# A fused forward and backward kernel with its order planned in advance: first loads, first norm, PSUM places of the last stage and output stores changed

## The chip, the cores and the metric

The kernel runs on one core of a Trainium2 chip. A core has TensorE (PE, matrix products into PSUM), VectorE (DVE), ScalarE (ACT), GpSimd (POOL) and SyncE (SP, which here only issues transfers). PSUM, where PE writes, is 128 partitions wide and is used here as eight places (banks) of 2 KB in each partition. Working memory beside it is one large "slab" that the kernel divides itself. Transfers are carried out by 16 DMA engines; they are issued on the queues of SP, ACT or POOL.

The metric is the device time of one execution in microseconds (us), the median of several runs. A profile is one such execution, recorded instruction by instruction; its span goes from the first to the last instruction.

## The reference

All arrays are bf16; the sequence has S = 2048 tokens of D = 512 channels, the hidden width is F = 1376. The forward pass normalizes the tokens and uses the result twice, in a long convolution and in a gated layer:

```python
xn = _layernorm(q)
k_shift = sum of 4 shifted copies of k, each times one tap of shift_k (per channel)
kv = k_shift * v
y  = irfft(rfft(kv padded to 4096) * rfft(ssm_k padded to 4096))[:2048] + kv * ssm_D
s  = xn * y
h  = sigmoid(xn @ w_gate) * (xn @ w_up)
out = q + s * silu(h @ w_down)
```

The result is `out` and the gradients of q, k, v, shift_k, ssm_k, ssm_D, w_gate, w_up and w_down for a given `grad_out`, so ten outputs (`out_0` to `out_9`).

## The kernel before, in words

**Tiles and stages.** Tokens are handled in 8 groups of 256 (`q` in the code), channels in 4 groups of 128 (`cg`). The Fourier transform of 4096 points is done by small matmuls (`step1n`, `step3` forward, `inv3`, `inv3w`, `inv1`, `inv1n` back). There are three stages:

1. Three streams side by side: `strG` (norm of the tokens in `f_ln`, its transposes in `f_Tpe` and `f_T`, gate and up products in `f_gen`), `strK` (the filter's transform) and `strV` (the four taps on k as matmuls with diagonal matrices `dg4`, the product with v, its transform, the product with the filter's and the way back).
2. `stepB`: the gated layer's output and its backward pass, token group by token group.
3. Behind the last groups of it: `dW` (the three weight gradients, in blocks of 16 matmuls of 128x512, 128x352 or 128x320 that accumulate in one PSUM place each), `frontC` (transform of the convolution's incoming gradient) and `backC` with `taps` (products with the stored transforms, the way back, and the gradients of k, v, the taps and the filter). `dW` reads chunks of stored activations by transposing loads on SP's queue; `backC` reads stored transforms (`KK_d`).

**The order.** The functions don't issue instructions. They record them in `Rec`, with what each depends on. `run_streams` interleaves the streams' records by a share of progress, and `Rec.order` then lays out all engines' instructions with estimated durations: at each step the engine that is free first takes the lowest-numbered recorded operation that is ready. PSUM tiles get their place there. A tile has a kind, and `KINDS` (L175) lists the sets of places that a kind may take; of the free sets the one that has been free longest is taken, and an operation whose tile finds none is put back. For a four-place tile that finds none, the planner holds places as they come free. The kinds that matter here:

- `m2`: two places, (4,5), (6,7), (2,3) or (0,1); used by `step1n` (L794), `step3` (L815) and `inv1` (L856), and by much of stages 1 and 2.
- `f4`: four places, 0 to 3 or 4 to 7; used by `inv3w` (L827), `inv3` (L841) and `inv1n` (L871).
- `f4a`: 0 to 3 alone. No tile of the kernel before has this kind.
- `hi`: one of 4 to 7; the accumulators of `dW`.
- `m1`: any single place.

The result is one fixed program; each engine works through its part in that order and waits at semaphores.

**The first microseconds.** `f_x(0)` (L939) loads the first 256 tokens as two halves of 64 partitions on SP's queue, and the first gate and up weights go out on ACT's queue behind nothing (L940). `gen_fft_consts` records the Fourier matrices' angles on DVE in two halves of a loop, and their sines on ACT; the generator hands over behind the loop. Then `f_ln(0)` is recorded: for each of two 128-token tiles statistics, their aggregate, an add of the epsilon, a power of -0.5 on POOL, and the normalizing product. `f_Tpe(0)` transposes by matmul. The rest of the constants waits for the second tile's statistics by an added dependency (`ln0`), the second group's norm for the first one's end. The diagonal matrices `dg4` of channel group 0 (L1062) need the taps, which POOL loads.

**The last outputs.** The gradient of v (`out_3`) is a product in `taps` for each channel group, in place in `y2A`; the gradient of k (`out_2`) is in `stC["v"]`. Both are stored behind the last channel group, in four row groups of two halves each: eight stores for each output, all 512 columns at a time.

In the profile nearly every instruction carries line L566 (PE) or L568 (all others), where recorded operations are issued, so groups are told apart by engine, operation and shape.

Of the kernel before, what the change touches and what calls it, by code (L numbers as in the profile page):

```python
# [17 lines left out]
P = 128  # L18
# [6 lines left out]
NJ = 16  # L25
# [138 lines left out]
class Rec:  # L164
# [8 lines left out]
    hold = None  # L173
    ENGS = ("tensor", "vector", "scalar", "gpsimd", "sync")
    KINDS = {"f4": [(0, 1, 2, 3), (4, 5, 6, 7)], "m2": [(4, 5), (6, 7), (2, 3), (0, 1)],  # L175
             "g2": [(4, 5), (6, 7), (2, 3)], "z2": [(4, 5), (6, 7)], "f4a": [(0, 1, 2, 3)], "lo": [(0,), (1,), (2,), (3,)],
             "hi": [(4,), (5,), (6,), (7,)], "m1": [(7,), (6,), (5,), (4,), (3,), (2,), (1,), (0,)]}

    def __init__(self, nc, tc, slab, psum):
# [418 lines left out]
def gen_fft_consts(nc, ar, negpi, Cn, TT, RT, I32):  # L598
    sc = 2 * math.pi / 8192
    rings = []  # L600

    def tmp(shape, dt):
        r = Ring(ar, shape, dt)
        rings.append(r)
        return r.ap
    a = tmp([16], i32)
    nc.gpsimd.iota(a, pattern=[[1, 16]], base=0, channel_multiplier=32)
    b = tmp([64], i32)
    nc.gpsimd.iota(b, pattern=[[2, 64]], base=1, channel_multiplier=0)
    pi_ = tmp([4], i32)  # L610
    nc.gpsimd.iota(pi_[:, 0:1], pattern=[[0, 1]], base=0, channel_multiplier=1)
    x32 = tmp([32], f32)
    nc.gpsimd.iota(x32, pattern=[[1, 32]], base=0, channel_multiplier=0, allow_small_or_imprecise_dtypes=True)
    yield
    nc.vector.tensor_single_scalar(a[64:128], a[64:128], -2032, ALU.add)
    m = tmp([8, 64], i32)
    mc = tmp([16, 2, 2, 32], i32)
    mv = m.rearrange("p j (h l) -> p j h l", h=2)
    for j in (slice(0, 8), slice(8, 16)):
        nc.vector.tensor_tensor(m, a[:, j, None].to_broadcast([P, 8, 64]), b[:, None, :].to_broadcast([P, 8, 64]), ALU.mult)  # L620
        nc.vector.tensor_single_scalar(mc[:, j, :, 1], mv, 8191, ALU.bitwise_and)
        nc.vector.tensor_single_scalar(m, m, 6144, ALU.add)
        nc.vector.tensor_single_scalar(mc[:, j, :, 0], mv, 8191, ALU.bitwise_and)
        nc.scalar.activation(Cn[:, j], mc[:, j].rearrange("p j h c l -> p j (h c l)"), ACT.Sin, bias=negpi, scale=sc)
    yield
    nc.vector.tensor_single_scalar(pi_[:, 1:2], pi_[:, 0:1], 31, ALU.bitwise_and)
    nc.vector.tensor_single_scalar(pi_[:, 2:3], pi_[:, 0:1], 5, ALU.arith_shift_right)
    nc.vector.tensor_single_scalar(pi_[:, 2:3], pi_[:, 2:3], 1, ALU.bitwise_and)
    pf = tmp([4], f32)
    nc.vector.tensor_copy(pf[:, 0:2], pi_[:, 1:3])  # L630
    nc.vector.tensor_scalar(pf[:, 2:3], pf[:, 1:2], -8.0, 24.0, ALU.mult, ALU.add)
    nc.vector.tensor_single_scalar(pf[:, 3:4], pf[:, 1:2], 24.0, ALU.mult)
    nc.vector.tensor_scalar(I32, x32, pf[:, 0:1], None, ALU.is_equal)
# [12 lines left out]
    for r in rings:  # L646
        r.free()
    yield
# [11 lines left out]
def kernel_impl(ctx, tc, A_q, A_k, A_v, A_shift_k, A_ssm_k, A_ssm_D, B_x, B_w_gate, B_w_up, B_w_down,  # L660
# [66 lines left out]

    T = [dict() for _ in range(8)]
    flags = set()


    def f_x(q):
# [2 lines left out]

    def f_ln(q):
        xq = T[q]["xq"]
        for t in range(2):
            i = 2 * q + t
            st = lnst.next()  # L740
            nc.vector.bn_stats(st[:, 0:6], xq[:, t])
            nc.vector.bn_aggr(st[:, 6:8], st[:, 0:6])
            nc.vector.tensor_scalar_add(st[:, 8:9], st[:, 7:8], LN_EPS)
            nc.gpsimd.tensor_tensor(out=rstd_all[:, i:i + 1], in0=st[:, 8:9], in1=neghalf, op=ALU.pow)
            nc.vector.tensor_scalar(xnA[:, i, :], xq[:, t], st[:, 6:7], rstd_all[:, i:i + 1], ALU.subtract, ALU.mult)

    def f_T(q):
        T[q]["xnT"] = xnT_r.next()
# [41 lines left out]
    def step1n(src):  # L790
        V = V_r.next()
        Vv = V.rearrange("p w (r j) e -> p r j w e", r=2)
        for jq in range(4):
            ps = nc.ps("m2", [2, 4, GW], f32)  # L794
# [17 lines left out]

    def step3(U, X):
        for c in range(2):
            ps = nc.ps("m2", [2, 16, 32], f32)  # L815
            calls = []
            for t in range(4):
                for k in range(2):
# [5 lines left out]
            nc.evac(X[:, c].rearrange("p (x k l) -> p x k l", k=2, l=32), ps[:].rearrange("p k x l -> p x k l"), 1024)  # L824

    def inv3w(parts, u, B):
        ps = nc.ps("f4", [2, 8, 2, 64], f32)  # L827
        calls = []
        for w in range(8):
            for n, (Y, R) in enumerate(parts):  # L830
# [22 lines left out]

    def inv1(B, dst):
        for jq in range(4):
            ps = nc.ps("m2", [2, 4, GW], f32)  # L856
            calls = []
            for j in range(4 * jq, 4 * jq + 4):
                for c in range(2):
# [8 lines left out]
            yield 4096  # L868

    def inv1n(B, dst):  # L870
        ps = nc.ps("f4", [32, 64], f32)  # L871
        for jh in range(2):
            for j8 in range(2):
                calls = []
# [61 lines left out]
    nc.gpsimd.memset(wu[:, :, F:FP], 0.0)  # L936
    nc.vector.memset(negpi, -math.pi)
    nc.vector.memset(neghalf, -0.5)
    f_x(0)  # L939
    ld_w(nc.scalar, 0, 512)  # L940
    nc.gpsimd.dma_start(skT, A_shift_k.rearrange("(cg p) t -> p cg t", p=P))
    nc.gpsimd.dma_start(Dcol_b, A_ssm_D.rearrange("(cg p) -> p cg", p=P))
# [8 lines left out]
    for op in rec.ops[n0:]:  # L951
        op.deps.add(n0 - 2)
    next(consts)
    ln0 = len(rec.ops) + 5
    f_ln(0)
    f_Tpe(0)
    f_x(2)
    n0 = len(rec.ops)
# [20 lines left out]
    def strG():  # L979
        for q in range(8):  # L980
            if q == 0:
                n0 = len(rec.ops)
                f_ln(1)
                rec.ops[n0].deps.add(ln0 + 4)
                f_Tpe(1)
            if q + 2 < 8:
                f_ln(q + 2)
# [68 lines left out]
    def strV():  # L1056
        for cg in range(NG):
# [3 lines left out]
            kvt = vg[:, :, c0 % 256:c0 % 256 + GW]  # L1061
            nc.vector.tensor_tensor(dg4, ident[:, None, :].to_broadcast([P, 4, GW]),  # L1062
                                    skT[:, cg, :, None].to_broadcast([P, 4, GW]), ALU.mult)
            kTp = kTp_r.next()
            for r in range(2):
                o = 13 + 16 * r
# [341 lines left out]
    def taps(cg):  # L1408
# [10 lines left out]
        nc.vector.tensor_tensor(dkv, dkv, stC["ksh"], ALU.mult)  # L1419
        if cg + 1 < NG:  # L1420
            ld_ksh(cg + 1)
        else:
            for j in range(0, NJ, 4):
                dma2o(nc.sync, o3C[:, :, j:j + 4], y2A[:, j:j + 4])
        yield 512
        pa = nc.ps("m1", [4, 32], f32)
        calls = []
# [10 lines left out]
        for lag in range(4):  # L1438
# [6 lines left out]
                nc.vector.tensor_tensor(term, src, skl, ALU.mult)  # L1445
                nc.vector.tensor_tensor(dk, dk, term, ALU.add)
            yield 512
        if cg + 1 == NG:
            for j in range(0, NJ, 4):
                dma2o(nc.sync, o2C[:, :, j:j + 4], stC["v"][:, j:j + 4])  # L1450

    def endC():
        yield from backC()
# [15 lines left out]
    def gated(g, flag):  # L1469
        yield from g  # L1470
        flags.add(flag)
    live = run_streams([(gated(stepB(), "B"), 8 * 45056, 0.0, 1.0)], until=lambda: "d2" in flags)
    Lfree.append(L0_r)
    ld_L()
# [114 lines left out]
```

## Time and profile before

| what | value |
|---|---|
| median of 3 runs | 505.53 us (501.62 to 507.21) |
| the profiled execution | 500.71 us |
| its span | 498.9 us |
| mean granted TensorE clock in it | 0.986 |
| PE busy | 461.0 us, 92% of the span |
| DVE busy | 391.1 us, 78% |
| ACT busy | 276.6 us, 55% |
| POOL busy | 21.0 us, 4% |
| moved by DMA | 112.74 MB, mean 226 GB/s |

Shares of busy time are means over stages; the prediction goes by stages. In rows of the timeline the columns are start and busy time in us, engine, line, operation, what is written and read with shape and type, the count, and in brackets how long the engine was idle just before and what ended it. SPq, ACTq and POOLq are the queues' issuing instructions. In rows of grouped instructions the columns are busy us, mean ns of one, and idle time before them with what ended it.

### The profile page before, as it was taken

How to read it: one execution, taken by the hardware profiler on the slowest of the kernel's cores; microseconds unless marked ns; L12 is line 12 of the kernel's file. 1: busy time of each engine (PE TensorE's matmuls, PEld its weight loads, DVE VectorE, ACT ScalarE, POOL GpSimd, SP SyncE). 2: the span in 40 equal slices, each digit the busy share in tenths (PEclk: the TensorE clock that was granted, in tenths of full speed). 3: DMA queues.
4: the chain of work that ended last, by engine and by line, in shares of the span. 5: the costliest groups of instructions: out<-in, count | busy, mean ns of one | idle time of the engine just before them, and what ended most of it. 6: DMA issues, size and time to landing. Idle time of an engine off the chain costs nothing.

```text
span 498.9 us, 13661 instructions
## 1 busy us (share of the span) xinstructions
PE 461.0 (92%) x5862; PEld 303.7 (61%) x5895; DVE 391.1 (78%) x658; ACT 276.6 (55%) x346; POOL 21.0 (4%) x48
## 2 busy tenths in 40 slices
PE   3999989999999999999999999999899879969997
PEld 2686866686768655565566556445446556657665
DVE  6788979758867499978998998649777779985870
ACT  5659798667665674255355267146556745254121
POOL 4010110000000000000000000100000000000000
PEclk9799999999999999999999999999989999998999
DMA  9999989927399897998969788996989998984666
GB/s 251 214 258 290 298 226 266 276 111 223 146 269 260 209 265 129 293 279 261 285 195 267 197 197 208 218 264 225 180 214 250 248 204 235 221 190 140 163 211 203
DMA packets 173813, 112.74 MB, mean 226 GB/s; under 512 B 101621, under 2 KB 157881, under 8 KB 173752
## 3 DMA queue, kind: packets, MB, share of 16 engines
q1 hardware_dynamic: 172344, 110.42, 87.0%
q10 hardware_dynamic: 1056, 1.05, 0.8%
q8 instruction: 46, 0.75, 0.6%
q0 software_dynamic: 352, 0.40, 0.3%
q14 instruction: 15, 0.12, 0.1%
HBM read 39.23 MB, written 47.62 MB: 174 GB/s over the span
## 4 chain that ended last, share of the span: by engine, by line
PE 71%; DVE 12%; issue 6%; ACT 6%; DMA 4%; POOL 1%; ACTq 0%; DVEq 0%; POOLq 0%
PE psum L566 71%; DVE slab L568 12%; ACT slab L568 6%; DMA slab<-slab 3%; DMA slab<-in_A_shift_k_dram 1%; POOL slab L568 1%; PE psum L568 0%; ACTq L568 0%; DVEq L568 0%; POOLq L568 0%; POOLq L1573 0%
## 5 line engine op out<-in xcount | busy, mean ns | idle before, releaser
L566 PE MATMUL psum<-slab 64*128 64x128 bf16 (+10 forms) x5853 | 459.6, 266 | 34.5 <-ACT slab L568 16.9
L566 PEld LDWEIGHTS <-slab 128*128 128x128 bf16 (+5 forms) x5886 | 303.0, 103 | 190.5 <-issue 55.7
L568 ACT CAST slab<-psum 128x1024 bf16<-128x1024 f32 (+4 forms) x265 | 218.2, 875 | 170.5 <-PE psum L566 153.6
L568 DVE TENSOR_TENSOR slab<-slab 128x1024 bf16<-128x1024 bf16 (+4 forms) x344 | 242.8, 758 | 30.6 <-ACT slab L568 12.7
L568 DVE CAST slab<-psum 128x1024 bf16<-128x1024 f32 (+1 forms) x29 | 34.1, 1183 | 28.4 <-PE psum L566 14.8
L568 ACT ACTIVATE slab<-psum 128x1024 bf16<-128x1024 f32 (+2 forms) x44 | 37.4, 855 | 30.3 <-PE psum L566 28.9
L568 DVE TENSOR_TENSOR slab<-psum,slab 128x1024 bf16<-128x1024 f32 (+2 forms) x28 | 28.1, 1004 | 16.6 <-PE psum L566 14.1
L568 DVE STREAM_TRANSPOSE slab<-slab 128x512 f32<-128x512 f32 x48 | 30.8, 684 | 3.4 <-ACT slab L568 3.2
L568 ACT ACTIVATE slab<-slab 128x512 bf16<-128x512 bf16 (+3 forms) x25 | 21.8, 889 | 16.9 <-DVE slab L568 16.8
L568 DVE SCALAR_TENSOR_TENSOR slab<-slab 128x512 bf16<-128x512 bf16 (+1 forms) x48 | 24.7, 529 | 3.8 <-ACT slab L568 3.4
L568 DVE TENSOR_SCALAR slab<-slab 128x1 f32<-128x1 f32 (+8 forms) x58 | 14.0, 270 | 2.6 <-POOL slab L568 1.8
L568 POOL TENSOR_TENSOR slab<-slab 128x1 f32<-128x1 f32 (+1 forms) x20 | 9.9, 508 | 74.9 <-DVE slab L568 66.9
L568 POOL MEMSET slab<- 128x128 bf16 (+3 forms) x7 | 3.1, 446 | 219.6 <-PE psum L566 176.2
L568 DVE BATCH_NORM_STATS2 slab<-slab 128x6 f32<-128x512 bf16 x16 | 10.3, 677 | 1.9 <-DMA slab<-in_A_q_dram 1.9
L568 POOL DMA_DIRECT2D slab<-slab x8 | 4.3, 536 | 148.6 <-DVE slab L568 148.6
L568 DVE SCALAR_TENSOR_TENSOR slab<-psum,slab 128x512 bf16<-128x512 f32 x10 | 6.7, 684 | 3.2 <-PE psum L566 3.2
L568 DVE COPY slab<-slab 128x1216 bf16<-128x1216 bf16 (+2 forms) x17 | 7.2, 441 | 0.0
L568 ACT ACT_TABLE_LOAD x2 | 2.6, 1283 | 1.8 <-issue 1.8
L568 DVE MEMSET slab<- 32x192 uint32 (+3 forms) x8 | 1.3, 165 | 1.9 <-PEq L1573 0.8
L568 DVE BATCH_NORM_AGGREGATE slab<-slab 128x2 f32<-128x6 f32 x16 | 2.5, 170 | 0.0
L568 PE MATMUL psum<-slab 128*4 128x128 bf16 (+1 forms) x9 | 1.7, 331 | 0.0
L568 POOL DMA_DIRECT2D slab<-in_A_shift_k_dram x2 | 1.5, 762 | 3.2 <-DMA sF_d<-slab 3.2
(15 smaller groups left out, 9.6 us busy)
## 6 DMA issues: line engine op xcount, KB each, us to landing
KK_d<-slab SPq DMA_DIRECT2D x16, 512.0 KB, 3.7
slab<-KK_d SPq DMA_DIRECT2D x16, 512.0 KB, 4.7
out_dram<-slab SPq DMA_DIRECT2D x58, 128.0 KB, 3.5
hS_d<-slab SPq DMA_DIRECT2D x8, 704.0 KB, 6.2
dgS_d<-slab SPq DMA_DIRECT2D x8, 704.0 KB, 5.9
duS_d<-slab SPq DMA_DIRECT2D x8, 704.0 KB, 5.4
sF_d<-slab SPq DMA_DIRECT2D x6, 704.0 KB, 5.3
slab<-sF_d SPq DMA_DIRECT2D x6, 704.0 KB, 6.1
```

What stands on the lines that cost most here:

```text
L566: getattr(self.nc.tensor, m)(*[place(v) for v in aa], **{x: place(v) for x, v in kk.items()})
L568: getattr(getattr(self.nc, eng), meth)(*[place(v) for v in a], **{x: place(v) for x, v in k.items()})
```

## The change

It has four parts, and helpers for them.

- *First loads.* The two halves of the first 256 tokens are issued as the first transfer on SP's queue and the first on ACT's.
- *First norm.* `f_ln` handles its two tiles together: both statistics, then both aggregates and adds (the sum with the epsilon now goes into `rstd_all` itself), one power for two columns on POOL, and two products. The constants' generator hands over in the middle of its loop too, and its second half is recorded behind `f_ln(0)`. `dg4` of channel group 0 gets a dependency on the first norm's last product. The numbers added to `ln0` follow the new order inside `f_ln`; they name the same operations as before (second tile's statistics, last product).
- *PSUM places of the last stage.* `step1n`, `step3` and `inv1` take their kind from `two["k"]`: `m2` as before in stage 1, and a new kind `c2`, (6,7), (2,3) or (0,1), for what is recorded from `stepB` on. `inv3w` and `inv1n` take `f4a`.
- *Stores in column halves.* `taps` stores 256 columns of both outputs behind each second channel group, in two row groups of two halves: four stores of 256 KB for each output behind channel group 1 and four behind group 3.

```diff
+            "c2": [(6, 7), (2, 3), (0, 1)], "g2": [(4, 5), (6, 7), (2, 3)], ...
...
         nc.scalar.activation(Cn[:, j], mc[:, j].rearrange("p j h c l -> p j (h c l)"), ACT.Sin, bias=negpi, scale=sc)
-    yield
+        yield
...
+    two = {"k": "m2"}
...
     def f_ln(q):
         xq = T[q]["xq"]
+        r = rstd_all[:, 2 * q:2 * q + 2]
+        st = [lnst.next() for t in range(2)]
         for t in range(2):
-            i = 2 * q + t
-            st = lnst.next()
-            nc.vector.bn_stats(st[:, 0:6], xq[:, t])
-            nc.vector.bn_aggr(st[:, 6:8], st[:, 0:6])
-            nc.vector.tensor_scalar_add(st[:, 8:9], st[:, 7:8], LN_EPS)
-            nc.gpsimd.tensor_tensor(out=rstd_all[:, i:i + 1], in0=st[:, 8:9], in1=neghalf, op=ALU.pow)
-            nc.vector.tensor_scalar(xnA[:, i, :], xq[:, t], st[:, 6:7], rstd_all[:, i:i + 1], ALU.subtract, ALU.mult)
+            nc.vector.bn_stats(st[t][:, 0:6], xq[:, t])
+        for t in range(2):
+            nc.vector.bn_aggr(st[t][:, 6:8], st[t][:, 0:6])
+            nc.vector.tensor_scalar_add(r[:, t:t + 1], st[t][:, 7:8], LN_EPS)
+        nc.gpsimd.tensor_tensor(out=r, in0=r, in1=neghalf.to_broadcast([P, 2]), op=ALU.pow)
+        for t in range(2):
+            nc.vector.tensor_scalar(xnA[:, 2 * q + t, :], xq[:, t], st[t][:, 6:7], r[:, t:t + 1], ALU.subtract, ALU.mult)
...
 (step1n, step3, inv1)
-            ps = nc.ps("m2", ...)
+            ps = nc.ps(two["k"], ...)
 (inv3w, inv1n)
-        ps = nc.ps("f4", ...)
+        ps = nc.ps("f4a", ...)
...
-    f_x(0)
+    T[0]["xq"] = xq_r.next()
+    for eng, r in ((nc.sync, 0), (nc.scalar, 1)):
+        eng.dma_start(T[0]["xq"][64 * r:64 * r + 64], qC[r, :, 0:2, :])
     ld_w(nc.scalar, 0, 512)
...
     next(consts)
-    ln0 = len(rec.ops) + 5
+    ln0 = len(rec.ops) + 1
     f_ln(0)
+    next(consts)
     f_Tpe(0)
...
                 f_ln(1)
-                rec.ops[n0].deps.add(ln0 + 4)
+                rec.ops[n0].deps.add(ln0 + 7)
...
             nc.vector.tensor_tensor(dg4, ...)
+            if cg == 0:
+                rec.ops[-1].deps.add(ln0 + 7)
...
 (taps)
         if cg + 1 < NG:
             ld_ksh(cg + 1)
-        else:
-            for j in range(0, NJ, 4):
-                dma2o(nc.sync, o3C[:, :, j:j + 4], y2A[:, j:j + 4])
+        if cg % 2 == 1:
+            for j in range(0, NJ, 8):
+                dma2o(nc.sync, o3C[:, :, j:j + 8, c0 - GW:c1], y2A[:, j:j + 8, c0 - GW:c1])
...
-        if cg + 1 == NG:
-            for j in range(0, NJ, 4):
-                dma2o(nc.sync, o2C[:, :, j:j + 4], stC["v"][:, j:j + 4])
+        if cg % 2 == 1:
+            for j in range(0, NJ, 8):
+                dma2o(nc.sync, o2C[:, :, j:j + 8, c0 - GW:c1], stC["v"][:, j:j + 8, c0 - GW:c1])
...
+    two["k"] = "c2"
     live = run_streams([(gated(stepB(), "B"), 8 * 45056, 0.0, 1.0)], until=lambda: "d2" in flags)
```

More of the change, by code (lines that the diff above doesn't have):

```diff
@@ L175 @@
     KINDS = {"f4": [(0, 1, 2, 3), (4, 5, 6, 7)], "m2": [(4, 5), (6, 7), (2, 3), (0, 1)],
-             "g2": [(4, 5), (6, 7), (2, 3)], "z2": [(4, 5), (6, 7)], "f4a": [(0, 1, 2, 3)], "lo": [(0,), (1,), (2,), (3,)],
+             "c2": [(6, 7), (2, 3), (0, 1)], "g2": [(4, 5), (6, 7), (2, 3)], "z2": [(4, 5), (6, 7)], "f4a": [(0, 1, 2, 3)], "lo": [(0,), (1,), (2,), (3,)],
              "hi": [(4,), (5,), (6,), (7,)], "m1": [(7,), (6,), (5,), (4,), (3,), (2,), (1,), (0,)]}
@@ L793, in step1n @@
         for jq in range(4):
-            ps = nc.ps("m2", [2, 4, GW], f32)
+            ps = nc.ps(two["k"], [2, 4, GW], f32)
             calls = []
@@ L814, in step3 @@
         for c in range(2):
-            ps = nc.ps("m2", [2, 16, 32], f32)
+            ps = nc.ps(two["k"], [2, 16, 32], f32)
             calls = []
@@ L826, in inv3w @@
     def inv3w(parts, u, B):
-        ps = nc.ps("f4", [2, 8, 2, 64], f32)
+        ps = nc.ps("f4a", [2, 8, 2, 64], f32)
         calls = []
@@ L855, in inv1 @@
         for jq in range(4):
-            ps = nc.ps("m2", [2, 4, GW], f32)
+            ps = nc.ps(two["k"], [2, 4, GW], f32)
             calls = []
@@ L870, in inv1n @@
     def inv1n(B, dst):
-        ps = nc.ps("f4", [32, 64], f32)
+        ps = nc.ps("f4a", [32, 64], f32)
         for jh in range(2):
```

## The prediction

> **What bounds the kernel now.** I read the page's totals first, then a table of stages, then the order in time of the two stages that the change touches. The totals and the chain of work that ended last:
>
> ```profile
> span 498.9 us, 13661 instructions
> PE 461.0 (92%) x5862; PEld 303.7 (61%) x5895; DVE 391.1 (78%) x658; ACT 276.6 (55%) x346; POOL 21.0 (4%) x48
> PE 71%; DVE 12%; issue 6%; ACT 6%; DMA 4%; POOL 1%; ACTq 0%; DVEq 0%; POOLq 0%
> ```
>
> TensorE (PE) is busy for 461.0 of 498.9 us, so a step gains if it fills PE's 37.9 us of idle time or shortens the end behind PE. The table of stages (span, PE, weight loads, DVE, ACT and POOL busy, then clock, DMA share, GB/s) says where that time lies:
>
> ```profile
> 0.00:14.00 14.00, 4.58 (x136) 3.61 (x136) 9.96 (x39) 8.06 (x9) 5.75 (x19) 0.91 0.94 257
> 14.00:100.00 86.00, 81.33 (x1283) 61.30 (x1286) 72.69 (x129) 65.05 (x72) 8.80 (x18) 0.97 1.03 260
> 395.00:448.00 53.00, 43.66 (x750) 29.85 (x750) 47.58 (x60) 27.48 (x37) 2.16 (x4) 1.00 0.98 215
> 461.00:499.00 38.00, 34.46 (x294) 22.91 (x292) 19.27 (x22) 7.49 (x18) 1.06 (x2) 1.00 0.68 192
> ```
>
> PE idles 9.4 us in the first 14 us and 9.3 us in 395 to 448, and 4.7 in the 86 us between 14 and 100. The two large holes are where the change works. From 461 us PE is busy but for the last 3.5 us.
>
> **The start.** The order in time, from the first load to the first matmuls of the gate:
>
> ```profile
> 0.75 1.23 SPq L568 DMA_DIRECT2D slab<-in_A_q_dram  x2
> 4.60 1.41 DVE L568 TENSOR_SCALAR slab<-slab 128x512 int32<-128x512 int32 x3
> 7.11 3.73 ACT L568 CAST slab<-psum 128x1024 bf16<-128x1024 f32 x4
> 7.91 1.29 DVE L568 BATCH_NORM_STATS2 slab<-slab 128x6 f32<-128x512 bf16 x2 [1.89 <-DMA slab<-in_A_q_dram]
> 9.11 0.16 DVE L568 BATCH_NORM_AGGREGATE slab<-slab 128x2 f32<-128x6 f32 x1
> 10.03 0.69 DVE L568 TENSOR_TENSOR slab<-slab 128x512 bf16<-128x512 bf16 x1 [0.76 <-DMA slab<-in_A_shift_k_dram]
> 10.64 0.15 DVE L568 TENSOR_SCALAR slab<-slab 128x1 f32<-128x1 f32 x1
> 10.87 1.25 POOL L568 TENSOR_TENSOR slab<-slab 128x1 f32<-128x1 f32 x3 [5.54 <-DVE slab L568]
> 11.95 0.61 PE L566 MATMUL psum<-slab 128*128 128x128 bf16 x4 [3.24 <-DVE slab L568]
> 12.59 0.59 ACT L568 CAST slab<-psum 128x512 bf16<-128x512 f32 x1 [1.75 <-PE psum L566]
> 14.39 5.82 PE L566 MATMUL psum<-slab 128*128 128x128 bf16 x48 [0.68 <-ACT slab L568]
> 18.04 2.67 SPq L568 DMA_TRANSPOSE slab<-in_A_k_dram  x1
> ```
>
> The reader sees DVE wait 1.89 us for the tokens, then, inside the norm, 0.76 us at the taps' product (10.03), whose operand comes by a slow POOL load. The norm's small steps and the power on POOL (10.87) queue behind it. PE waits 3.24 us for all of this.
>
> *Two queues.* The two token loads take SP 1.23 us together, 0.6 each; the second goes to ACT's queue. It removes at least that: stats at 7.3. DVE's integer work ends at 6.01 (4.60 + 1.41), so they can't start before 6.0. I take the middle, 6.7. Two weight loads on ACT's queue start one issue later, about 0.5 us; the gate's matmuls need them only behind 11 us. The Trainium skill, "DMA: Bandwidth & Descriptors", section "Rules for kernel authors", speaks against this: two transfers to disjoint partition halves share the same engines, and a second queue saves only the sequencer's issue time. By it the stats start at 7.3 and the sum below shrinks by 0.2 us; no run here shows the split yet.
>
> *The product behind the norm, and one power for two tiles.* The norm's own steps, by form:
>
> ```profile
> L568 POOL TENSOR_TENSOR slab<-slab 128x1 f32<-128x1 f32 x16 | 9.2, 586 | 66.9 <-DVE slab L568 66.9
> L568 DVE TENSOR_SCALAR slab<-slab 128x512 bf16<-128x512 bf16 x2 | 0.8, 408 | 0.0
> ```
>
> From the stats: 1.29, two aggregates and two adds 0.64 (2 x 0.16 + 2 x 0.15, rounded up), one power 0.59, the first product 0.41, four hand-overs of about 0.05: 3.13 us, so the first normalized tile is there at 9.83. PE transposes to 10.49; ACT's four casts (7.11 + 3.73) end at 10.84, so the casts run 10.84 to 12.02 and the gate starts at 12.07 in place of 14.39: **-2.3 us** (stats at 7.3 put the second cast at 12.3 and give -2.0; stats at 6.0 with ACT free give -3.3). A power of two columns isn't in the trace; one column has 0.59 and I take that, twice it at most. The moved taps' product (0.69) now lies beside PE; its reader is the taps' matmul, which also needs the keys, whose transposing load goes out at 18.04, so it is hidden. Splitting the constants' step adds no instruction. For the other 14 tiles the merged norm drops seven powers from a POOL that is 4% busy, and makes a tile wait for its neighbour: 0, between -4.1 (seven powers of 0.59, were each on the path) and +4.5 (seven neighbours' stats of 0.65).
>
> Does the gain last? Behind it PE is busy 81.33 of 86 us, with DMA at 1.03. What is late next are the keys and the last weights. I keep three quarters: **-1.8** (bounds 0 and -3.3).
>
> *The clock.* The granted clock halves behind PE's first hole:
>
> ```profile
> 10.00:12.00 2.00, 0.05 (x1) 0.06 (x2) 1.90 (x12) 0.84 (x1) 1.13 (x3) 0.88 1.09 340
> 14.00:18.00 4.00, 3.61 (x25) 3.05 (x26) 2.19 (x5) 2.54 (x4) 0.17 (x1) 0.50 1.09 265
> 448.00:452.00 4.00, 4.00 (x150) 3.77 (x140) 1.29 (x2) 2.95 (x3) 0.00 (x0) 0.57 1.08 197
> ```
>
> From 14.39 to 18 PE runs at 0.50, which costs up to 1.8 us (half of 3.6). I leave this as it is: the hole is shorter by 2 us but the transposes stay thin. At 448 to 452 the same follows the second hole; 4 us at 0.57 cost up to 1.7, and I take half, **-0.8**, if that hole is filled.
>
> **The last stage.** PE beside ACT, and then all PE forms from 437 to 448:
>
> ```profile
> 396.65 3.80 ACT L568 CAST slab<-psum 128x1024 bf16<-128x1024 f32 x4 [0.18 <-PE psum L566]
> 399.58 7.07 PE L566 MATMUL psum<-slab 128*128 128x352 bf16 x152 [1.79 <-ACT slab L568]
> 442.87 1.96 PE L566 MATMUL psum<-slab 64*128 64x128 bf16 x64 [1.10 <-DVE slab L568]
> 446.87 0.25 PE L566 MATMUL psum<-slab 64*64 64x128 bf16 x4 [2.04 <-ACT slab L568]
> 447.79 11.48 PE L566 MATMUL psum<-slab 64*64 64x128 bf16 x372 [0.67 <-ACT slab L568]
> ```
>
> ```profile
> L566 PE MATMUL psum<-slab 128*128 128x320 bf16 x17 | 2.8, 300 | 0.0
> L566 PE MATMUL psum<-slab 64*64 64x64 bf16 x128 | 2.4, 193 | 0.0
> L566 PE MATMUL psum<-slab 64*128 64x128 bf16 x64 | 2.0, 216 | 1.1 <-DVE slab L568 1.1
> L566 PE MATMUL psum<-slab 64*64 64x128 bf16 x20 | 0.7, 222 | 2.7 <-ACT slab L568 2.7
> ```
>
> At 399.58 a weight-gradient block (128x352) waits for ACT although its operands are old: its PSUM place is still being emptied. From 437 to 448 one block ends (x17) and no new one starts, though the next chunk was requested long before:
>
> ```profile
> 416.56 7.58 SPq L568 DMA_TRANSPOSE slab<-duS_d  x1
> 428.70 6.33 SPq L568 DMA_TRANSPOSE slab<-duS_d  x1
> ```
>
> These blocks may use places 4 to 7 only, and the four-place inverse tiles may lie in 0 to 3 or 4 to 7. With two inverse tiles open no block can start (the trace shows no places; this is read from the code). The change keeps inverse tiles in 0 to 3 and step tiles off 4 and 5, so a block always finds room. The holes that it can fill are 1.79 + 1.10 + 2.04 + 0.67 = 5.6 us. I take four fifths, **-4.4** (from -9.3, all idle time of the stage, to 0 where the blocks are held by something else, or a loss: rival three). The holes named "issue" stay.
>
> What it costs: a second inverse tile now waits for the first's two casts, 3.80/4 = 0.95 each, 1.9 us. PE can do a block meanwhile. The filter chain, however, ends later, and DVE's taps hang on it. DVE's products for one inverse tile, its last taps, and ACT's last cast:
>
> ```profile
> 443.98 3.88 DVE L568 TENSOR_TENSOR slab<-slab 128x2048 bf16<-128x2048 bf16 x5 [0.49 <-PE psum L566]
> 476.82 7.52 DVE L568 TENSOR_TENSOR slab<-slab 128x2048 bf16<-128x2048 bf16 x6
> 495.54 0.43 ACT L568 CAST slab<-psum 128x320 bf16<-128x320 f32 x1 [1.75 <-PE psum L566]
> ```
>
> DVE ends at 484.34, PE's last cast at 495.97, 2.9 us ahead of the span's end.
>
> *Column halves.* Of sixteen 256 KB stores, eight move ahead to the second filter group (about 425 to 445 us), and runs shrink from 4096 to 512 bytes. Two rows price them, loads with 512-byte runs and the late stores:
>
> ```profile
> L568 SPq DMA_DIRECT2D slab<-in_A_v_dram x12: 477/626/1305, 20.8 to 391.0; - x12
> out_dram<-slab SPq DMA_DIRECT2D x13, 256.0 KB, 4.1
> ```
>
> Eight issues of 0.63 hold SP for 5.0 us, in two lots of 2.5, ahead of the next transposes and filter loads. SP waits in order, so a store whose product is late delays these too. The chunks are fetched a block ahead, which hides 2.5 us; without that cover PE loses up to 5.0. I take 0 (bounds +5 and -1, for the freer end). At the end half of the last output remains: DVE's end plus 4 x 0.63 plus 4.1 is 6.6 us.
>
> **Sum.** -1.8 - 4.4 - 0.8 = -7.0 us. The profiled execution took 500.71 us, 1.8 beside its span; it would take 493.7. The median of the runs shown is 505.53, 4.8 above it; the same step from there gives **498.5**.
>
> **Rivals.**
> 1. *The start stays at full clock as well* (10%). The Trainium skill, "TensorE: Matmul & The Clock Gate", section "The HAM clock gate (the "warmup" mystery)", says that the clock is halved after an idle window of about 3.4 us. The trace agrees so far: 3.24 us idle, then 0.50. If the shorter hole keeps the clock, the 1.8 us come off too: 496.7.
> 2. *Only the start pays* (20%). Blocks are bound by the order of the filter work, not by room; PE's waits on DVE and ACT at 442 to 448 are data. Against it: the x17 row. -1.8 gives 503.7.
> 3. *The change doesn't do what it says* (11%): the halves land no sooner, ACT's casts hold the start, and the holes move: 505.5.
> 4. *Slower: the filter chain becomes the end* (19%). Sixteen inverse tiles share one place. If eight of them wait 1.9 us on DVE's path, DVE ends at 484.34 - 1.8 + 15.2 = 497.7; plus 6.6 the span is 504.3, 5.4 more: 510.9. It decides once DVE's end passes 485.3 (PE's new end, 495.97 + 2.9 - 7.0 = 491.9, less 6.6), which is 2.8 us of delay. DVE is busy 47.58 of 53 us from 395 to 448, which speaks for it; that the products for one inverse tile take DVE 3.88 us, twice the casts, against it.
>
> The forecast has the other 40%.
>
> **Chances and range.** A measurement of this kernel tells about 1%, 5 us, from no change. Faster by that (below 500.5): most of the forecast (33), rival one (10) and a little of rival two (3), 0.46. Slower (above 510.6): two thirds of rival four with some of three, 0.15. The same: 0.39. The range goes from 493 (the larger ends of the start, the clock and the stage's holes) to 511 (rival four).
>
> **What would show it.** In the profile after: stats at 6.0 to 7.3 and the gate's first matmul near 12; the taps' product behind the normalized tiles; 352-wide blocks between 437 and 448 and no PE wait on ACT ahead of a block; clock 1.00 behind it; output stores at 425 to 445; DVE's last product ahead of PE's last matmul. Wrong, if PE's idle time from 395 to 448 stays near 9.3 us, if DVE or a store ends last, or if what the start gains is idle time again by 100 us.

## The result and the profile after

The changed kernel took 500.39 us (median of 20 runs), the kernel before 503.25 us beside it (20 runs). The ratio is 0.9926, with a 95% interval of 0.9900 to 0.9951: 3.7 us faster, about half of the 7.0 us forecast (the two medians lie 2.9 us apart). That is within 1%, what the prediction calls the same, though the interval lies clear of 1; 500.4 us lies inside 493 to 511. Ratios here leave out executions more than 1.5% above the fastest of their kernel, and as all three profiled executions of the changed kernel are such (505.26 us in the one shown), the mechanisms below are read stage by stage and the sizes taken from the ratios.

The start, in order of time (columns as in the prediction's rows):

```profile
0.75 0.60 SPq L568 DMA_DIRECT2D slab<-in_A_q_dram  x1
0.75 0.56 ACTq L568 DMA_DIRECT2D slab<-in_A_q_dram  x1
5.93 1.28 DVE L568 BATCH_NORM_STATS2 slab<-slab 128x6 f32<-128x512 bf16 x2
7.70 0.73 POOL L568 TENSOR_TENSOR slab<-slab 128x2 f32<-128x2 f32 x1 [2.37 <-DVE slab L568]
9.62 0.69 DVE L568 TENSOR_TENSOR slab<-slab 128x512 bf16<-128x512 bf16 x1
11.22 0.68 DVE L568 COPY slab<-slab 128x2048 bf16<-128x2048 bf16 x1
11.96 4.28 PE L566 MATMUL psum<-slab 128*128 128x128 bf16 x27 [1.84 <-DVE slab L568]
```

The two halves go out at the same moment; the statistics begin at 5.93 with no wait for the tokens (7.91, behind 1.89 us of waiting, before). The edit does two things here: it splits the load, and it puts the second half ahead of the first weight load on ACT's queue, which goes out at 1.35 us in place of 0.74. In the kernel before the weights moved ahead of the tokens: up to 5.5 us ACT's queue (q10 in the profile) had moved 0.81 MB and SP's (q1) 0.13 MB, and the tokens landed 6.4 us after their issue. The columns of the first two rows are packets, MB and share of the DMA engines; the third row ends with KB each and us from issue to landing:

```profile
q10 hardware_dynamic: 804, 0.81, 59.2%
q1 hardware_dynamic: 80, 0.13, 7.5%
slab<-in_A_q_dram SPq DMA_DIRECT2D x2, 128.0 KB, 6.4
```

In the changed kernel the half on SP's queue lands after 3.6 us. No run separates the split from the place ahead of the weights.

The taps' product, at 9.62, waits for nothing, and PE's long run of matmuls starts at 11.96 in place of 14.39. In both kernels this run begins with sixteen matmuls of the filter's transform, which wait for DVE's copy of 128x2048 (until 14.33 before, 11.90 now). The gate's own matmuls, 256 columns wide, follow at 13.68 in place of 16.11.

The table of stages (span, PE, weight loads, DVE, ACT and POOL busy, then clock, DMA share, GB/s):

```profile
14.00:18.00 4.00, 4.00 (x26) 2.47 (x25) 1.27 (x2) 2.88 (x3) 0.18 (x1) 1.00 1.09 239
340.00:395.00 55.00, 47.57 (x877) 28.63 (x880) 41.08 (x56) 33.86 (x39) 0.00 (x0) 0.99 0.97 226
395.00:448.00 53.00, 49.75 (x742) 32.75 (x740) 44.61 (x57) 25.88 (x36) 2.16 (x4) 0.95 0.91 217
448.00:461.00 13.00, 10.70 (x290) 8.01 (x290) 6.88 (x8) 6.96 (x9) 0.00 (x0) 1.00 0.98 203
461.00:503.50 42.50, 33.29 (x398) 22.07 (x395) 25.25 (x30) 8.23 (x18) 2.12 (x4) 0.95 0.66 150
```

Two of these stretches of the kernel before are not in the prediction:

```profile
340.00:395.00 55.00, 50.22 (x896) 29.95 (x900) 42.36 (x58) 35.08 (x41) 0.00 (x0) 0.97 0.95 222
448.00:461.00 13.00, 12.53 (x381) 10.05 (x370) 6.58 (x8) 6.34 (x7) 1.06 (x2) 0.87 0.58 134
```

The hole in 395 to 448 is filled: PE is busy for 49.75 of 53 us, 43.66 before. But PE idles 7.4 us in the 55 us ahead of it (4.8 before), 2.3 us in the 13 us behind it (0.5 before), and 9.2 us from 461 on, where it had 3.5. What fills the hole, PE's forms from 437 to 448 (busy us, mean ns):

```profile
L566 PE MATMUL psum<-slab 128*128 128x352 bf16 x26 | 4.2, 313 | 0.0
L566 PE MATMUL psum<-slab 128*128 128x320 bf16 x26 | 3.7, 299 | 0.0
```

These are matmuls of the weight gradients' blocks, 52 where there had been 17.

The end, first SP, DVE's last products and ACT's last cast, then one step of the chain of work that ended last (start, length, what), and last the same seven products in the kernel before:

```profile
465.59 6.92 SPq L568 DMA_TRANSPOSE slab<-duS_d  x1
465.82 1.07 POOL L568 DMA_DIRECT2D slab<-slab  x2 [38.69 <-DVE slab L568]
473.31 8.66 DVE L568 TENSOR_TENSOR slab<-slab 128x2048 bf16<-128x2048 bf16 x7 [4.14 <-DMA slab<-slab]
474.20 25.25 SPq L568 DMA_DIRECT2D out_dram<-slab  x21
485.52 7.52 DVE L568 TENSOR_TENSOR slab<-slab 128x2048 bf16<-128x2048 bf16 x6
496.15 0.42 ACT L568 CAST slab<-psum 128x320 bf16<-128x320 f32 x1 [1.75 <-PE psum L566]
```

```profile
466.35 6.93 DMA slab<-slab
```

```profile
463.67 8.65 DVE L568 TENSOR_TENSOR slab<-slab 128x2048 bf16<-128x2048 bf16 x7 [3.78 <-DMA out_dram<-slab]
```

DVE's products now end at 493.04 (484.34 before), and the span ends 6.9 us behind ACT's last cast (2.9 before). On the chain stands a small transfer within the slab, a shift that POOL issues for the filter chain: 6.93 us, beside a transposing load issued 0.23 us ahead of it. But this wait isn't what makes DVE later than before: the kernel before waits 3.78 us at the same place, by its profile for an output store, and DVE comes to that place at 469.2 in place of 459.9. The waits from 340 us on, added up by what ended them (total us, times, longest), show what changed. After:

```profile
DVE slab L568 <- ACT slab L568: 17.7, 11, 4.2
DVE slab L568 <- PE psum L566: 11.1, 7, 2.9
...
PE psum L566 <- ACT slab L568: 0.5, 1, 0.5
```

Before:

```profile
DVE slab L568 <- ACT slab L568: 11.1, 8, 3.3
DVE slab L568 <- PE psum L566: 6.0, 6, 1.8
...
PE psum L566 <- ACT slab L568: 5.8, 5, 2.0
```

PE's waits on ACT are gone (5.8 to 0.5 us) and DVE's on ACT and PE have grown by 11.7 us (its other waits fell from 10.1 to 4.8). PE's waits of all kinds haven't shrunk in this execution, though: 14.7 us, 14.2 before.

### The profile page after: what moved, and what is told of

The parts are those of the page before. It is cut to its first block, busy times and chain, and to the rows that moved or that the text cites. A ratio compares the mean times of both kernels' runs of the same rounds, so it can differ in the third digit from the quotient of the medians.

```text
span 503.5 us, 13650 instructions
## 1 busy us (share of the span) xinstructions
PE 464.2 (92%) x5862; PEld 304.1 (60%) x5895; DVE 396.4 (79%) x663; ACT 272.7 (54%) x341; POOL 20.9 (4%) x40
## 4 chain that ended last, share of the span: by engine, by line
PE 61%; issue 13%; DMA 3%; DVE 3%; ACT 2%; POOL 0%; ACTq 0%; POOLq 0%
PE psum L566 61%; DMA slab<-slab 3%; DVE slab L568 3%; ACT slab L568 2%; PE psum L568 0%; POOL slab L568 0%; ACTq L568 0%; POOLq L568 0%
## 5 line engine op out<-in xcount | busy, mean ns | idle before, releaser
L566 PE MATMUL psum<-slab 128*128 128x256 bf16 (+10 forms) x5853 | 462.8, 266 | 31.9 <-issue 10.9
L568 ACT CAST slab<-psum 128x1024 bf16<-128x1024 f32 (+4 forms) x260 | 214.0, 874 | 170.9 <-PE psum L566 146.7
L568 DVE CAST slab<-psum 128x1024 bf16<-128x1024 f32 (+2 forms) x34 | 39.5, 1170 | 37.4 <-PE psum L566 20.3
L568 DVE TENSOR_TENSOR slab<-psum,slab 128x1024 bf16<-128x1024 f32 (+2 forms) x28 | 28.2, 1008 | 13.2 <-PE psum L566 10.4
L568 POOL TENSOR_TENSOR slab<-slab 128x2 f32<-128x2 f32 (+1 forms) x12 | 9.8, 821 | 79.6 <-DVE slab L568 69.9
L568 DVE BATCH_NORM_STATS2 slab<-slab 128x6 f32<-128x512 bf16 x16 | 10.4, 679 | 1.3 <-DMA slab<-in_A_q_dram 1.3
```

The source lines that it names most:

```text
L566: getattr(self.nc.tensor, m)(*[place(v) for v in aa], **{x: place(v) for x, v in kk.items()})
L568: getattr(getattr(self.nc, eng), meth)(*[place(v) for v in a], **{x: place(v) for x, v in k.items()})
```

## The experiments

Two theories were set against each other. **A**: the start pays; the last stage's holes are filled, but the filter chain, with the taps and the stores behind it, then sets the end. **B**: the places pay in full, and what the start gains is lost by 100 us. All ratios are to the kernel before on the same chip.

| kernel | ratio | 95% interval |
|---|---|---|
| whole change again, three times | 0.9926, 0.9965, 0.9954 | 0.9900–0.9951, 0.9926–1.0003, 0.9920–0.9989 |
| start alone | 0.9933 | 0.9896–0.9970 |
| places alone | 1.0125 | 1.0084–1.0166 |
| change without column halves | 1.0035 | 0.9997–1.0073 |
| start and halves | 0.9945 | 0.9911–0.9979 |
| only `f4a` | 1.0048 | 1.0011–1.0084 |
| only `c2` | 1.0078 | 1.0044–1.0112 |
| change, last stores on POOL's queue | 0.9915 | 0.9876–0.9955 |
| start, `f4a`, halves, POOL's queue | 0.9885 | 0.9829–0.9942 |

### The change again, and each half of it

The whole change, unaltered:

> The changed kernel once more, beside the three below, for a second profile. Theory A (the start pays, the holes of the last stage are filled, and then the filter chain with the taps and the last output stores sets the end, so that most of what the places gained is given back): 3 to 5 us less than before, PE waiting less than 5 us in 395 to 448 us, DVE's last product at 488 us or later, and 5 us or more from PE's last cast to the end of the span. Theory B (the places pay in full, the start's gain is lost by 100 us): the same time, but an end set by PE, 3 us behind its last cast.

Measured: 501.78 us against 502.89, 0.9965, less than theory A's 3 to 5 us; PE's waiting from 395 to 448 (4.2 us), DVE's end (491.19) and the 6.8 us behind PE's last cast are as A says. The start alone:

```diff
-    two["k"] = "c2"
...
-        ps = nc.ps("f4a", ...)
+        ps = nc.ps("f4", ...)
...
(both outputs' stores as in the kernel before)
```

> Only the start's parts on the kernel before: first halves on two queues, merged norm, split constants, product behind the norm; m2 and f4 places and row stores as before. Theory A: 2 to 4 us less than before (the gate at 12 us in place of 14.4, clock 1.00 up to 20 us). Theory B: within 1 us of before.

Measured: 498.98 against 502.89, 0.9933, or 3.4 us. The end of stage two is marked by DVE's last product of `stepB`. First the kernel before, then the start alone:

```profile
324.84 0.43 DVE L568 TENSOR_TENSOR slab<-slab 128x512 bf16<-128x512 bf16 x1
```

```profile
11.84 12.38 PE L566 MATMUL psum<-slab 128*128 128x128 bf16 x122 [2.18 <-ACT slab L568]
...
321.90 0.42 DVE L568 TENSOR_TENSOR slab<-slab 128x512 bf16<-128x512 bf16 x1
```

PE's long run is 2.55 us earlier (14.39 to 11.84), and 310 us later the lead is 2.94 us. It isn't so in every execution: with the same start this product comes at 322.15 in the repeat of the change and at 324.98, no lead at all, in the execution shown first. Over the eight profiled executions with the new start it comes at 323.1 on average, over the four with the old one (the kernel before and three variants below) at 325.8: 2.7 us. The timed 3.4 us (1.5 to 5.2 by the interval) agree: the lead lasts, and B's second half falls. The places alone:

```diff
+            "c2": [(6, 7), (2, 3), (0, 1)],
...
+    two["k"] = "c2"
...
-        ps = nc.ps("f4", ...)
+        ps = nc.ps("f4a", ...)
```

> Only the PSUM places of the last stage on the kernel before (c2 and f4a). Theory A: 0 to 2 us less than before, as DVE's last product moves from 484 to 488 us or later and half of 4 MB of row stores stands behind it. Theory B: 4 to 5 us less. Rival four of the prediction in full: 5 us more.

Measured: 508.15 against 502.89, 1.0125, or 6.3 us slower: neither A's 0 to 2 us less nor B's 4 to 5, but what rival four gives in full. Its stage row, its waits from 340 us on, SP, DVE and ACT at the end:

```profile
395.00:448.00 53.00, 49.27 (x775) 33.18 (x775) 45.21 (x58) 27.44 (x37) 2.16 (x4) 1.00 0.97 212
```

```profile
DVE slab L568 <- ACT slab L568: 21.4, 12, 5.6
```

```profile
470.47 31.82 SPq L568 DMA_DIRECT2D out_dram<-slab  x28
485.10 7.52 DVE L568 TENSOR_TENSOR slab<-slab 128x2048 bf16<-128x2048 bf16 x6
494.81 0.43 ACT L568 CAST slab<-psum 128x320 bf16<-128x320 f32 x1 [1.02 <-DMA out_dram<-slab]
```

The holes are filled (49.27 of 53 us). This execution came 2.2 us late out of stage two; counted from there PE's last matmul ends 4.4 us earlier than before, and ACT's last cast, which now waits for a store, 3.0 us (at 495.24). The waits from 340 us on show the exchange: PE's of all kinds fall from 14.2 to 10.0 us, DVE's rise from 27.2 to 31.2, those on ACT from 11.1 to 21.4. DVE ends at 492.62, 6.0 us later than before if counted from the end of stage two, and the span ends 13.8 us behind its last product and 11.1 behind the last cast. SP issues the last of its 28 stores only at 502. B's first half falls too.

### The column halves

The change with the stores as in the kernel before:

```diff
-        if cg % 2 == 1:
-            for j in range(0, NJ, 8):
-                dma2o(nc.sync, o3C[:, :, j:j + 8, c0 - GW:c1], ...)
+        else:
+            for j in range(0, NJ, 4):
+                dma2o(nc.sync, o3C[:, :, j:j + 4], y2A[:, j:j + 4])
(o2C alike)
```

> The change without the column halves: start and places changed, both outputs stored as whole rows behind the last channel group. Theory A: 1 to 4 us more than the full change, since 2 MB in place of 1 MB is to be stored behind DVE's last product. Theory B, or halves that cost as much as they bring: within 1 us of the full change.

Measured: 504.39, 1.0035, 0.7% behind the whole change on the same chip. Then the start with the halves, without the places:

```diff
(start alone, and:)
+        if cg % 2 == 1:
+            for j in range(0, NJ, 8):
+                dma2o(nc.sync, o3C[:, :, j:j + 8, c0 - GW:c1], ...)
(o2C alike)
```

> The start's parts and the column halves, without the PSUM places. With the start alone PE's last cast came at 492.7 us, 11.6 us behind DVE's last product, so the row stores stood behind no one. Theory A (the halves are worth something only where DVE ends late): the same as the start alone within 2 us, 3 us less than before. Rival (moving half of the stores to the middle frees the end of the span anyway): 2 us or more less than the start alone.

Measured: 498.83 against 502.08, 0.9945, the same as the start alone (0.9933). So the halves show no worth by themselves and about 0.7% where the places have made DVE late (each of the two ratios is known within 0.4%): they pay back part of what the places cost. The rows of the kernel without them show what they save and what they cost:

```profile
453.24 6.61 SPq L568 DMA_TRANSPOSE slab<-duS_d  x1
466.72 1.07 POOL L568 DMA_DIRECT2D slab<-slab  x2 [43.53 <-DVE slab L568]
492.26 0.43 ACT L568 CAST slab<-psum 128x320 bf16<-128x320 f32 x1 [0.81 <-DMA out_dram<-slab]
```

Its span of 504.2 us ends 11.5 us behind this cast, that of the whole change 6.8 to 6.9: the halves save 4.7 us there. Its last transposing load goes out 13 us ahead of the shift at 466.72, which lands undisturbed. With the halves SP comes to this load later, at 463 to 468, just ahead of the shift.

### The two kinds of places

```diff
(only f4a, on the kernel before: inv3w, inv1n)
-        ps = nc.ps("f4", ...)
+        ps = nc.ps("f4a", ...)
```

> On the kernel before, inverse tiles in places 0 to 3 alone; step tiles as before. Theory: one place for inverse tiles is what delays the filter chain, so nearly all of the 6 us that both place edits cost together appear here: DVE's last product at 490 us or later, DVE waiting 17 us or more for ACT from 340 us on (11.1 before, 21.4 with both), 4 to 6 us more than before. Rival (the step tiles' three pairs delay it): within 2 us of before.

Measured: 504.40 against 502.08, 1.0048, or 2.4 us: DVE ends late and waits as expected, but the time lies between theory and rival.

```diff
(only c2, on the kernel before: step1n, step3, inv1)
-            ps = nc.ps("m2", ...)
+            ps = nc.ps(two["k"], ...)
...
+    two["k"] = "c2"
```

> On the kernel before, step tiles kept off places 4 and 5; inverse tiles as before. Theory (the inverse tiles' one place is the cost): within 2 us of before, DVE's last product at 483 to 487 us. Rival (the three pairs): 4 to 6 us more.

Measured: 505.98 against 502.08, 1.0078, or 3.9 us, again between theory and rival, and DVE's last product ends at 489.58, late as well. Each of the two costs by itself, and the costs add up to that of both (0.48 + 0.78 = 1.26%, measured 1.25%, each within 0.4%). Their ways differ. The stages with `c2` alone, then the waits and the end with `f4a` alone:

```profile
340.00:395.00 55.00, 45.53 (x871) 26.98 (x866) 43.11 (x58) 32.08 (x37) 0.00 (x0) 1.00 0.95 220
...
448.00:461.00 13.00, 9.85 (x386) 7.97 (x387) 9.30 (x13) 8.72 (x10) 1.06 (x2) 1.00 0.86 183
```

```profile
DVE slab L568 <- ACT slab L568: 17.0, 11, 3.3
```

```profile
482.01 7.51 DVE L568 TENSOR_TENSOR slab<-slab 128x2048 bf16<-128x2048 bf16 x6
491.78 0.43 ACT L568 CAST slab<-psum 128x320 bf16<-128x320 f32 x1 [0.82 <-DMA out_dram<-slab]
```

With `c2` the hole of 395 to 448 is filled as with the others (49.23 of 53 us), and as much idle time stands just beside it: 9.5 us in 340 to 395 (4.8 before) and 3.2 in 448 to 461 (0.5 before). The hole has moved, and PE sets the end: its last cast lasts until 501.22, its last matmul ends 175.3 us behind the end of stage two (170.6 before). With `f4a` PE is done early (last cast until 492.21) and DVE pays: its last product ends at 489.52, 4.0 us later than before if counted from the end of stage two.

### The last stores on another queue

SP waits in order. In the whole change four 256 KB stores stand on it behind stores of weight gradients, which wait for PE. In the repeat of the change DVE's last product ends at 491.19 and SP issues the four between 494.6 and 498.1. So they were given to POOL's queue, which is idle then:

```diff
-                dma2o(nc.sync, o2C[:, :, j:j + 8, c0 - GW:c1], ...)
+                dma2o(nc.gpsimd if cg + 1 == NG else nc.sync, o2C[:, :, j:j + 8, c0 - GW:c1], ...)
```

> The full change, but the last four stores of the gradient of k go out on POOL's queue. In the changed kernel SP issued them 4 us behind DVE's last product, since a weight-gradient store that waits for PE stands ahead of them in SP's order. Theory (SP's order holds them): the span ends 3 to 4 us behind PE's last cast in place of 6.8, and the time is 2 to 4 us below the full change. Rival (their transfer itself is the length): within 1 us of the full change.

Measured: 498.61 against 502.08, 0.9915. Its rows:

```profile
463.74 6.23 SPq L568 DMA_TRANSPOSE slab<-duS_d  x1
463.80 1.07 POOL L568 DMA_DIRECT2D slab<-slab  x2 [39.16 <-DVE slab L568]
467.14 8.65 DVE L568 TENSOR_TENSOR slab<-slab 128x2048 bf16<-128x2048 bf16 x7
487.99 2.79 POOL L568 DMA_DIRECT2D out_dram<-slab  x4 [10.81 <-DVE slab L568]
492.25 0.43 ACT L568 CAST slab<-psum 128x320 bf16<-128x320 f32 x1 [1.75 <-PE psum L566]
```

POOL issues the four 0.3 us behind DVE's last product, and the span (497.1) ends 4.4 us behind the last cast in place of 6.8: 2.4 us by the queue. By time this gain isn't shown, as the interval of 0.9915 overlaps those of the whole change. The rest of the difference between the profiles, some 4 us, has another cause: here the shift lands at once and DVE's seven products start at 467.14 without a wait. In the repeat of the change the same shift leaves at 463.80 as well, but the transposing load is 0.70 us ahead of it in place of 0.06, and DVE waits 4.31 us:

```profile
463.10 6.12 SPq L568 DMA_TRANSPOSE slab<-duS_d  x1
463.80 1.07 POOL L568 DMA_DIRECT2D slab<-slab  x2 [39.10 <-DVE slab L568]
471.46 8.66 DVE L568 TENSOR_TENSOR slab<-slab 128x2048 bf16<-128x2048 bf16 x7 [4.31 <-DMA slab<-slab]
```

Whether the new queue or chance set this distance of 0.06 us isn't known.

Both findings together, start, `f4a`, halves and POOL's queue without `c2`, beside the whole change once more:

```diff
(the kernel above, without:)
-    two["k"] = "c2"
```

> The start's parts, inverse tiles in places 0 to 3, column halves, the last four stores of the gradient of k on POOL's queue; step tiles with all four pairs of places as before. Theory: counted from the end of the second stage, the inverse tiles' places alone brought PE's end 6 us forward and cost 2.5 us at the span's end by late stores, the three pairs of the step tiles cost both; so with the late stores out of SP's order this takes 2 to 5 us less than the full change with POOL's stores, 6 to 9 us less than before. Rival (what one place change gives, DVE's chain takes back): within 1 us of the full change with POOL's stores, 3 to 5 us less than before.

> The changed kernel once more, for a profile and beside the variant above. By the runs so far 2 to 4 us less than before.

Measured: 499.40 against 504.28, 0.9885 (six runs), and 501.52, 0.9954. The variant's 5.8 us (2.9 to 8.6 by the interval) lie between expectation and rival. It is the fastest of all by ratio, but its interval (0.9829 to 0.9942) overlaps those of the start alone and of the kernel with the whole change and POOL's queue; that it beats either isn't shown. Its end confirms the queue's part: POOL issues at 494.65, DVE's end being 494.36, and the span of 503.5 us ends 4.0 us behind the cast, against 6.9 in the whole change beside it (span 509.6, cast until 502.64).

### The start taken apart

Only the split of the first loads, on the kernel before:

```diff
-    f_x(0)
+    T[0]["xq"] = xq_r.next()
+    for eng, r in ((nc.sync, 0), (nc.scalar, 1)):
+        eng.dma_start(T[0]["xq"][64 * r:64 * r + 64], qC[r, :, 0:2, :])
```

> Only the split of the first loads over SP's and ACT's queues, on the kernel before. Theory: statistics start at 5.9 us in place of 7.9, but DVE still waits for the taps near 10, so the gate starts within 0.5 us of 14.4 and the second stage ends within 1 us of 324.8.

Measured in one run: 505.35 us; span 503.5.

```profile
5.93 1.28 DVE L568 BATCH_NORM_STATS2 slab<-slab 128x6 f32<-128x512 bf16 x2
...
9.44 0.69 DVE L568 TENSOR_TENSOR slab<-slab 128x512 bf16<-128x512 bf16 x1 [1.75 <-DMA slab<-in_A_shift_k_dram]
```

The statistics come as early as in the whole change (5.93), so this gain is that of the two first loads alone. DVE, early now, waits 1.75 us at the taps' product, 0.76 before. Even so PE's long run starts at 11.79, not near 14.4 as expected; yet stage two ended at 325.1, no earlier than before. PE is busy 79.68 of the 86 us from 14 to 100, 81.33 before: in this execution most of the lead was idle time again by 100 us. The other way round, the start's parts with both halves on SP's queue:

```diff
(start alone, and:)
-    for eng, r in ((nc.sync, 0), (nc.scalar, 1)):
...
+    f_x(0)
```

> The start's parts without the split of the first loads. Theory: statistics at 7.9 as before, no wait for the taps inside the norm, the gate at about 13 us, and the second stage ends 1 to 2 us earlier than before. If the two parts only pay together the gate stays near 14.4.

Measured in one run: 514.24 us, span 512.5: the slowest kernel of all, though PE's long run starts at 12.46, 1.9 us earlier than before. Stage two ends 6.8 us late, where 1 to 2 us early was expected. PE has 3.1 us less work in the 52 us from 48 to 100 (45.38 in place of 48.50), and from 48 to 184 it waits 7.4 us on DVE where it had waited 2.5. The program is ordered anew for every variant, and two streams meet there in another order; what makes this order so much worse wasn't followed further. Both are single runs, and 505.35 us lies among the runs of the kernel before (500.57 to 508.09), so what either part of the start is worth by itself isn't shown.

## Why the prediction was right, and where only the total was

**The total came out of terms that were wrong in both directions.** The prediction has start −1.8, clock −0.8, places −4.4, halves 0: −7.0. By the timed ratios, on 503 us: start with its clock −3.4 (0.9933), places +6.3 alone and +5.1 on top of the start (1.0035 against 0.9933), halves −3.5 on top of both (0.9965 against 1.0035). These make −1.8, the whole change's 0.9965 on that chip; the first measurement gave −3.7. The range held because the errors cancel in part, and that is luck. That the places and the halves together gain anything over the start alone (0.9933) isn't shown.

**Start: the gain is there, its size too small, one row misread.** "Stats at 6.7" was 5.93: the halves land before DVE asks for them, so the lower bound of 6.0 was the case. "The gate starts at 12.07" takes the row at 14.39 for the gate's. That run begins with matmuls of the filter's transform, and these wait for DVE's copy; that it now starts at 11.96 (11.84 in the start alone), when the casts, done at 11.81, are just ready as well, is in part luck. The gate's own matmuls moved by 2.4 us, close to the forecast's 2.3. The two-column power took 0.73 us where 0.59 was taken. "I keep three quarters" failed: the lead of 2.55 us was 2.94 us at the end of stage two, and 3.4 us in the timed runs. The stats at 7.3, which the prediction works out from a second queue that saves only the issue time, were wrong: 2.0 us were saved (7.91 to 5.93), more than one issue of 0.6 us. This doesn't refute the rule of the Trainium skill ("DMA: Bandwidth & Descriptors", section "Rules for kernel authors") that it cites, since the edit also took the weight load from ahead of the tokens: 0.81 MB on ACT's queue against 0.13 MB on SP's up to 5.5 us.

**Clock: rival one did not come.** The row of 14 to 18 us shows 1.00 for the changed kernel, 0.50 before. But this trace has no record of the clock ahead of 18.0 us, and PE gets through only 26 matmuls in these 4 us, as the kernel before does at 0.50 (25 in 3.61 us). The gate's matmuls of 256 columns start 213 ns apart in both kernels there, and 109 ns apart once the clock is 1.00. Where the record is whole the clock is halved behind the shorter hole too: 0.50 from 12 to 14 us in the start alone, behind a wait of 2.18 us, and 0.50 from 13 to 16 in the repeat of the change, behind 1.99 us. So these traces don't bear out that a hole shorter than the window of about 3.4 us, which the prediction cited from the Trainium skill, "TensorE: Matmul & The Clock Gate", section "The HAM clock gate (the "warmup" mystery)", keeps the clock. What moved is the end of the slow stretch: 14.9 to 18.0 us in the eight executions with the new start, 18.3 to 20.0 in the four with the old one. Behind the filled hole the clock is 1.00 in 448 to 461 (0.87 before), as forecast, but it is 0.95 in 395 to 448 and from 461 on, where it had been 1.00: this term brought nothing in the profile.

**Places: the step that failed.** "The holes that it can fill ... I take four fifths, −4.4" is right for PE. In the places alone PE ended 4.4 us earlier, counted from the end of stage two (166.2 in place of 170.6); the blocks stand between 437 and 448; and PE's waits on ACT went. What failed is the step from PE's end to the span's end, and the weight given to it. Rival four named the mechanism (the inverse tiles share one place, DVE's chain is delayed, DVE's end decides once it passes 485.3) at 19%. It came true in the places alone (DVE's end 492.6) and in the changed kernel (493.0, and 491.2 in the repeat). What DVE lost is 6.0 us in the places alone, more than PE's 4.4, both counted from the end of stage two. The argument used against it, that DVE's products take twice ACT's casts, looked at one tile by itself; DVE's waits on ACT from 340 us on nevertheless rose by 10.3 us with the places alone. And rival four priced the inverse tiles alone; `c2`, which the prediction gave no cost, costs no less than `f4a` (0.78% and 0.48%, each within 0.4%) and does it through PE's own order.

**Halves: "I take 0 (bounds +5 and −1)" was the wrong value, and its lower bound was too narrow.** They bring about 3.5 us on top of start and places, where DVE ends late. The bound of −1 was worked out for the end as it was, with DVE done 11 us ahead of PE; with rival four's end the same stores are on the path, and the halves take half of them away. That the halved stores "delay these too" was seen as well, in another form: they push the last transposing load from 453 us (without halves) to 463 to 468, beside the shift.

**The end: "plus 6.6 for stores" was too short.** It counts issue and landing from DVE's end and takes SP to be free. In the changed kernel SP was held by stores that wait for PE, and the span ended 10.4 us behind DVE's last product.

**Left open.** Whether the wait at the shift (4.1 to 5.6 us) also occurs in the runs near the median: it stands in each profiled execution of the whole change, and no quicker one was profiled. That it makes part of the spread of 496.5 to 511.3 us is a guess. How `c2` leads the order to idle ahead of 395 us, and why the start without the split is slow, were not followed. Every variant is ordered anew as a whole, so a part's cost is that of the order it leads to; the 514.24 us of one variant show how far an order can stray.

## What to carry to other kernels

When an idle hole of the busiest engine is to be filled by letting other work in, follow the work that owned the hole to its last store: here PE won 4.4 us, and the chain that had held its places lost 6.0 us behind it. Let the engine with free time issue the last stores of a chain rather than an in-order queue that already holds stores waiting for another engine (here 2.4 us at the end of the profile; the time didn't show it). And time each part by itself as well as together: here the halves showed no worth alone and 0.7% with the part that hurts, and a total near the forecast hid two terms with the wrong sign or size. Before a granted clock of 1.00 is believed, count the matmuls in the stretch.

## What the runs showed of the hardware that was not expected

- Two halves of one 128-partition load, the first transfers on SP's and ACT's queues, had landed when DVE first asked, at 5.93 us (the one on SP's queue 3.6 us after its issue). Both on SP's queue, with a 512 KB weight load first on ACT's, they took 6.4 us in the kernel before, and DVE waited until 7.68 to 8.27 in five executions. Whether the split or the place ahead of the weights does it isn't separated.
- The same shift within the slab, two transfers of about 48 KB, took 1.7 to 2.6 us each where the last transposing load had been issued 5.6 us or more ahead, 2.4 and 2.8 with one issued 0.06 us ahead, and 4.0 to 8.4 us in five executions with one issued 0.23 to 3.4 us ahead (the last two shifts of each execution).
- A granted clock of 0.50 followed waits of PE of 1.99, 2.13 and 2.18 us at the start as well as one of 3.24 us.
- A power on POOL of 128x2 values took 0.73 us, of 128x1 0.59 us: two columns for a quarter more.
